# Two memory chains and two attention sweeps: from stages of their own to shared stages on five and three PSUM banks

## The chip, the cores and the metric

One core of a Trainium2 chip runs the whole program. The metric is the device time of one execution in microseconds (us). All executions told of here were fast, the undisturbed state. "Half clock" and "full clock" are the two values, 0.50 and 1.00, that the trace records for the clock granted to TensorE.

## The reference, cut to what matters

The program computes `g*a + (1-g)*b` for 2048 tokens of 576 features and the gradients of eleven inputs. Branch `a` is a plain attention with 32 heads of 18 features over one shared key and value. Branch `b` walks through 64 segments of 32 tokens, and each segment's eight memory rows are the output of the segment before.

```python
def _A_ref(x, wq, wk, wv, wo):
    q = (x @ wq) ...                       # 32 heads of 18
    k = x @ wk;  v = x @ wv                # one shared head
    p = softmax(q @ k.T * Dh ** -0.5)
    return (p @ v) ... @ wo
def _B_ref(x, mem0, Wq, Wk, Wv, Wo, seg_len):
    mem = mem0
    for s in range(n_seg):                 # 64 steps, strictly one after the other
        h = concatenate([mem, xs], axis=1) # 8 memory rows + 32 tokens
        q, k, v = ...                      # 32 heads of 128
        o = softmax(mask(q @ k.T)) @ v ... @ Wo
        mem = o[:, :M, :]
        outs.append(o[:, M:, :])
# out, vjp = jax.vjp(...): forward and all gradients
```

In the kernel the attention of `a` with its gradients is two *sweeps* of 1024 iterations each, an iteration being one 128x512 tile of scores for two heads. The memory recurrence of `b` is two *chains* of 64 steps, one forward and one backward. A sweep depends on no chain and a chain on no sweep.

## The kernel before

Each stage has its own pools, opened and closed one after the other, so no stage overlaps the next:

```python
                with SB("a2s") as a2s, PS("a2p") as a2p:
                    k.a_pass1(a1k, a2s, a2p)                 # first sweep
        with SB("a3k") as a3k, SB("a3s") as a3s, PS("a3p") as a3p:
            k.a_pass2(a3k, a3s, a3p)                         # second sweep
        # ... a_out, loads, b_proj_x cut ...
                with SB("cfs") as cfs, PS("cfp") as cfp:
                    k.b_chain_fwd(bw, cfs, cfp)              # forward chain
        # ... transposed weights, b_bulk cut ...
            with SB("rk") as rk, SB("rs") as rs, PS("rp") as rp:
                k.load_WoT(rk)
                k.b_chain_bwd(rk, rs, rp)                    # backward chain
```

One iteration of the first sweep. Its PSUM tiles come in pieces of 512 fp32 columns, one bank each, eight in all: three for S (the scores), two pairs for dP (the products with the output gradient) and one for the accumulator acc. E is the exponential of S, W the product of dP and E:

```python
                for kt in range(NTT):
                    k0 = kt * P
                    S = [psum.tile([P, 512], F32, name="a_S", bufs=3) for _ in range(2)]
                    dP = psum.tile([P, 2, 512], F32, name="a_dP", bufs=2)
                    for i in range(4):
                        r = slice(32 * i, 32 * i + 32)
                        dst = S[i][:, :] if i < 2 else dP[:, i - 2, :]
                        self.mm(dst, lhsT=self.KV[r, k0:k0 + P], rhs=QD[r, :], tp=(32 * i, 0))
                    Et = sp.tile([P, 2, 512], BF16, name="a_E", bufs=3)
                    Wt = sp.tile([P, 2, 512], BF16, name="a_W", bufs=3)
                    for i in range(2):
                        nc.scalar.activation(Et[:, i, :], S[i][:, :], ACT.Exp, scale=SCALEA)
                    nc.vector.tensor_tensor(out=Wt[:], in0=dP[:], in1=Et[:], op=ALU.mult)
                    # two acc matmuls of Et and two of Wt, 128x64 tiles side by side: cut
```

The second sweep is built alike, with b_S, b_dP, b_E, b_dS and four acc matmuls of 32 columns of the array. The last product of each backward chain step and the copies after it:

```python
            ph = psum.tile([P, 1024], F32, name="r_ph", bufs=1)
            for (lo, hi) in ((0, 512), (512, D)):
                for wi in (2, 0, 1):
                    for u in range(8):
                        for g in range(4):
                            self.mm(ph[32 * g:32 * g + 32, lo:hi], lhsT=dT[:, wi, u, :], rhs=self.WT[wi][:, 8 * g + u, lo:hi],
                                    start=(wi == 2 and u == 0), stop=(wi == 1 and u == 7), tp=(0, 32 * g))
            hs = sp.tile([P, D], F32, name="r_hs", bufs=1)
            nc.vector.tensor_copy(hs[:, 0:256], ph[:, 0:256])
            nc.scalar.copy(hs[:, 256:D], ph[:, 256:D])
```

The softmax here doesn't subtract the row's maximum and nothing guards it: scores larger than these inputs give would overflow.

## Time and profile before

The time is 11398.7 us (median of 4 runs, 11384.2 to 11406.1). The stages, from the first and last starts of their tiles:

| stage | us | per iteration or step | granted clock |
|---|---|---|---|
| first sweep | 2037 | 1.99 | 0.83 |
| second sweep | 1464 | 1.43 | 0.50 |
| forward chain | 1468 | 22.9 | 0.75 |
| bulk attention of branch b | 2000 | - | 0.59 |
| backward chain | 1545 | 24.1 | 0.65 |
| all the rest | 2891 | - | - |

The prediction below shows the lines that carry this. TensorE's timeline in the second sweep (start us, duration, engine, line, operation, tiles, shapes, count):

```profile
2600.48 0.60 PE L66 MATMUL b_dP<-b_KV,b_QD 32*128 32x512 bf16 x2
2600.49 0.96 PE L66 MATMUL b_S<-b_KV,b_QD 32*128 32x512 bf16 x2
2601.37 0.61 PE L66 MATMUL b_acc<-b_dS,b_SD 128*32 128x512 bf16 x2
2601.38 0.61 PE L66 MATMUL b_acc<-b_E,b_SD 128*32 128x512 bf16 x2
```

The eight matmuls of an iteration stand in two *groups*: four row tiles (dP and S) start together, then four column tiles (acc). Matmuls of one group share the array at the same time; each group takes over 0.5 us at half clock. A group is what the prediction calls a slot.

```profile
8496.58 8.82 PE L66 MATMUL r_ph<-WT,r_dT 128*32 128x512 bf16 x192 [0.46 <-ACT r_dT L608]
...
8507.59 3.74 PE L66 MATMUL r_pj<-WoT,dm 128*32 128x512 bf16 x40 [0.28 <-DVE dm L627]
```

After the product (r_ph) TensorE waits for two copies, and the next step's 40 projections (r_pj) then take 3.74 us.

### The profile page before, as it was taken

The numbers are of one execution on the slowest core, as the hardware profiler recorded it, in microseconds if no ns is written. First come the engines' busy times: TensorE is split into PE (matmuls) and PEld (weight loads), VectorE is DVE, ScalarE is ACT, GpSimd is POOL, SyncE is SP. The second block draws the span as 40 slices with busy tenths as digits, with TensorE's granted clock in tenths as the row PEclk, the third lists the DMA queues.
The fourth block names the chain that finished last, engine by engine and source line by source line (L and its number), as shares of the span: only waits on it lengthen the run. The fifth ranks groups of instructions, "written<-read, shape, count | busy, mean of one in ns | idle before, by whom it ended". The sixth has DMA issues, their size and how long they took to land. (4 is left out here: it accounts for less than half of the span.)

```text
span 11405.0 us, 219104 instructions
## 1 busy us (share of the span) xinstructions
PE 8865.9 (78%) x91009; PEld 3869.9 (34%) x91416; DVE 4143.1 (36%) x5742; ACT 3592.5 (31%) x6629; POOL 1540.5 (14%) x2664
## 2 busy tenths in 40 slices
PE   6777777799999998888876666665777776655898
PEld 2222222211112444444443333333333333333344
DVE  5666666688886331212122222221111111111001
ACT  4666666677776331111121111110000001112000
POOL 2111111100000000000022222221111111112101
PEclk8888888655556997777755655666666668877999
DMA  1000000311112442222254444444222224445544
GB/s 66 9 9 9 9 9 9 96 49 49 46 49 85 175 172 43 44 44 43 43 164 114 111 118 114 111 117 121 55 55 54 55 60 125 124 116 188 169 149 137
DMA packets 929961, 945.24 MB, mean 83 GB/s; under 512 B 457193, under 2 KB 801458, under 8 KB 910146
## 3 DMA queue, kind: packets, MB, share of 16 engines
q1 hardware_dynamic: 859330, 714.18, 21.7%
q0 software_dynamic: 69632, 217.01, 6.9%
q8 instruction: 716, 11.73, 0.4%
q14 instruction: 283, 2.32, 0.1%
HBM read 558.16 MB, written 372.57 MB: 82 GB/s over the span
## 5 line engine op out<-in xcount | busy, mean ns | idle before, releaser
L948 DVE TENSOR_TENSOR a_W<-a_dP,a_E 128x1024 bf16<-128x1024 f32 x1024 | 1252.4, 1225 | 583.3 <-ACT a_E L947 483.8
L1035 DVE TENSOR_TENSOR b_dS<-b_dP,b_E 128x1024 bf16<-128x1024 f32 x1024 | 1231.3, 1223 | 211.3 <-PE b_S L66 163.1
L947 ACT ACTIVATE a_E<-a_S 128x512 bf16<-128x512 f32 x2048 | 1116.0, 595 | 445.8 <-PE a_S L66 385.6
L1034 ACT ACTIVATE b_E<-b_S 128x512 bf16<-128x512 f32 x2048 | 1111.1, 594 | 351.0 <-DVE b_dS L1035 243.2
L66 PE MATMUL b_S<-b_KV,b_QD 32*128 32x512 bf16 x2048 | 897.8, 588 | 25.0 <-DMA b_QD<-qd_dram 25.0
L66 PE MATMUL a_acc<-a_W,a_WK 128*64 128x512 bf16 x2048 | 471.0, 447 | 387.5 <-DVE a_W L948 387.1
L66 PE MATMUL b_acc<-b_E,b_SD 128*32 128x512 bf16 x2048 | 626.9, 608 | 4.3 <-DMA b_SD<-sd_dram 3.3
L66 PE MATMUL b_acc<-b_dS,b_SD 128*32 128x512 bf16 x2048 | 626.2, 607 | 4.3 <-DVE b_dS L1035 1.8
L66 PE MATMUL b_dP<-b_KV,b_QD 32*128 32x512 bf16 x2048 | 620.7, 603 | 0.0
L66 PE MATMUL r_ph<-WT,r_dT 128*32 128x512 bf16 x12288 | 562.0, 353 | 29.5 <-ACT r_dT L608 29.5
L66 PE MATMUL a_S<-a_QD,a_KV 32*128 32x512 bf16 x2048 | 539.4, 443 | 44.6 <-ACT a_QD L922 43.1
L66 PE MATMUL w_acc<-w_d,w_h 128*128 128x512 bf16 (+1 forms) x2352 | 523.1, 380 | 37.5 <-DMA w_d<-dqx_dram 34.8
L66 PE MATMUL a_acc<-a_E,a_VK 128*64 128x512 bf16 x2048 | 520.2, 441 | 28.9 <-ACT a_E L947 25.8
L679 DVE COPY y_T<-y_pt 128x512 bf16<-128x512 bf16 x384 | 151.3, 422 | 934.8 <-PE y_pt L71 920.5
L66 PE MATMUL a_dP<-a_QD,a_KV 32*128 32x512 bf16 x2048 | 455.6, 441 | 0.0
L66 PE MATMUL y_pdx<-WT,y_T 128*128 128x64 bf16 (+1 forms) x2976 | 426.5, 289 | 24.1 <-ACT y_dx L685 10.9
L66 PEld LDWEIGHTS <-a_WK 128*64 128x64 bf16 x2048 | 195.1, 111 | 687.5 <-issue 680.0
L66 PE MATMUL c_pm<-c_oT,WoN 128*128 128x8 bf16 (+1 forms) x10080 | 340.3, 173 | 38.4 <-DVE c_oT L282 27.0
L66 PEld LDWEIGHTS <-r_dT 128*32 128x32 bf16 x12288 | 256.4, 109 | 334.9 <-issue 217.6
L66 PEld LDWEIGHTS <-b_SD 128*32 128x32 bf16 x4096 | 120.6, 101 | 731.1 <-issue 725.5
L66 PEld LDWEIGHTS <-WoN 128*128 128x128 bf16 (+1 forms) x10080 | 338.1, 114 | 50.9 <-issue 49.6
L66 PE MATMUL y_pk<-y_qB,y_dsB 128*128 128x512 bf16 x112 | 49.9, 446 | 391.9 <-DMA y_dsB<-dsmq_dram 391.9
(424 smaller groups left out, 13336.7 us busy)
## 6 DMA issues: line engine op xcount, KB each, us to landing
b_SD<-sd_dram SPq DMA_DIRECT2D x64, 512.0 KB
b_QD<-qd_dram SPq DMA_DIRECT2D x64, 512.0 KB
qx_dram<-p_tok SPq DMA_DIRECT2D x16, 1024.0 KB
qxT_dram<-p_tT SPq DMA_DIRECT2D x16, 1024.0 KB
kx_dram<-p_tok SPq DMA_DIRECT2D x16, 1024.0 KB
kxT_dram<-p_tT SPq DMA_DIRECT2D x16, 1024.0 KB
vx_dram<-p_tok SPq DMA_DIRECT2D x16, 1024.0 KB
vxT_dram<-p_tT SPq DMA_DIRECT2D x16, 1024.0 KB
```

The lines of the kernel that those rows point to most:

```text
L66: return self.nc.tensor.matmul(out, lhsT, rhs, start=start, stop=stop, tile_position=tp, skip_group_check=True)
L679: nc.vector.tensor_copy(tT[:], pt[:])
L947: nc.scalar.activation(Et[:, i, :], S[i][:, :], ACT.Exp, scale=SCALEA)
L948: nc.vector.tensor_tensor(out=Wt[:], in0=dP[:], in1=Et[:], op=ALU.mult)
L1034: nc.scalar.activation(Et[:, i, :], S[i][:, :], ACT.Exp, scale=SCALEA)
L1035: nc.vector.tensor_tensor(out=dS[:], in0=dP[:], in1=Et[:], op=ALU.mult)
```

## The change

Its intent: while a chain waits for softmaxes and copies, a sweep's independent matmuls can fill TensorE, so chain and sweep of each pair should cost little more than the larger of the two. The pools of a pair are open together, the chain is traced first and so goes first in the scheduler, and PSUM is split: three banks for the chain, five for the sweep.

```diff
+                with SB("a2k") as a2k, SB("cfs") as cfs, PS("cfp") as cfp, SB("a2s") as a2s, PS("a2p") as a2p:
+                    k.load_A_kv(a2k)
+                    k.b_chain_fwd(a2k, cfs, cfp)
+                    k.a_pass1(a2k, a2s, a2p)
 ... (cut)
-            with SB("rk") as rk, SB("rs") as rs, PS("rp") as rp:
+            with SB("rk") as rk, SB("rs") as rs, PS("rp") as rp, SB("a3k") as a3k, SB("a3s") as a3s, PS("a3p") as a3p:
                 k.load_WoT(rk)
                 k.b_chain_bwd(rk, rs, rp)
+                k.a_pass2(a3k, a3s, a3p)
 ... (in both sweeps; cut to the first)
-                    S = [psum.tile([P, 512], F32, name="a_S", bufs=3) for _ in range(2)]
-                    dP = psum.tile([P, 2, 512], F32, name="a_dP", bufs=2)
+                    S = [psum.tile([P, 512], F32, name="a_S", bufs=2) for _ in range(2)]
+                    dP = [psum.tile([P, 512], F32, name="a_dP", bufs=2) for _ in range(2)]
 ...
-                    nc.vector.tensor_tensor(out=Wt[:], in0=dP[:], in1=Et[:], op=ALU.mult)
+                    for i in range(2):
+                        nc.vector.tensor_tensor(out=Wt[i][:], in0=dP[i][:], in1=Et[i][:], op=ALU.mult)
 ... (last product of the backward step)
-            ph = psum.tile([P, 1024], F32, name="r_ph", bufs=1)
-            for (lo, hi) in ((0, 512), (512, D)):
+            for hf in range(2):
+                lo, hi = 288 * hf, 288 * hf + 288
+                ph = psum.tile([P, 288], F32, name="r_pj", bufs=2)
 ...
-            nc.vector.tensor_copy(hs[:, 0:256], ph[:, 0:256])
-            nc.scalar.copy(hs[:, 256:D], ph[:, 256:D])
+                nc.scalar.copy(hs[:, lo:hi], ph[:])
```

To make room, the rest was moved about: the Q and dO projections of the sweep became a stage of their own and are reloaded from memory; the output gradient's projection moved out of the bulk stage into the token projections; the second sweep loads 512 columns at a time; several tiles lost a buffer.

## The prediction

> **What bounds the kernel now.** I first read the page's busy shares (TensorE 78%, no other engine over 36%) and then the tiles' first and last starts, which split the run into stages. They run one after the other, so I asked for a table by stage. Columns: stretch, length, busy us of TensorE, weight loads, VectorE, ScalarE and GpSimd, then granted clock, DMA share, GB/s. In order: first sweep, second sweep, forward chain, bulk attention, backward chain.
>
> ```profile
> PEclk8888888655556997777755655666666668877999
> 113.00:2150.00 2037.00, 1482.96 (x9413) 467.27 (x9412) 1265.44 (x1088) 1298.36 (x2371) 298.18 (x808) 0.83 0.03 10
> 2150.00:3614.00 1464.00, 1434.15 (x8192) 254.56 (x8192) 1231.47 (x1026) 1113.17 (x2052) 13.30 (x24) 0.50 0.18 59
> 4250.00:5718.00 1468.00, 1259.27 (x24644) 694.34 (x24643) 291.86 (x643) 166.40 (x387) 132.55 (x190) 0.75 0.25 45
> 5830.00:7830.00 2000.00, 1321.80 (x9743) 725.16 (x9888) 502.57 (x1023) 360.96 (x656) 526.85 (x659) 0.59 0.43 119
> 7830.00:9377.00 1547.00, 1155.72 (x23752) 603.18 (x23751) 304.30 (x899) 116.36 (x320) 182.07 (x330) 0.65 0.27 56
> ```
>
> The sweeps use VectorE and ScalarE, the chains nearly only TensorE: the sum of a sweep and a chain is 3505 us (first pair) and 3011 us (second), and the change hopes to pay little more than the larger of each. Look at the clock: second sweep 0.50, with TensorE "busy" 98%. What sets an iteration there is VectorE:
>
> ```profile
> L948 DVE TENSOR_TENSOR a_W<-a_dP,a_E 128x1024 bf16<-128x1024 f32 x1024 | 1252.4, 1225 | 583.3 <-ACT a_E L947 483.8
> L1035 DVE TENSOR_TENSOR b_dS<-b_dP,b_E 128x1024 bf16<-128x1024 f32 x1024 | 1231.3, 1223 | 211.3 <-PE b_S L66 163.1
> L61 DVE CAST p_tok<-p_pb 128x512 bf16<-128x512 f32 x192 | 132.8, 692 | 327.4 <-PE p_pb L66 327.4
> ```
>
> 1.22 us of 1.43 us per iteration (1464/1024). Last, the timeline of TensorE, because the change alters how matmuls are grouped:
>
> ```profile
> 997.91 0.59 PE L66 MATMUL a_acc<-a_E,a_VK 128*64 128x512 bf16 x1 [0.26 <-ACT a_E L947]
> 998.43 0.60 PE L66 MATMUL a_S<-a_QD,a_KV 32*128 32x512 bf16 x1
> 998.96 0.64 PE L66 MATMUL a_acc<-a_E,a_VK 128*64 128x512 bf16 x1
> 999.53 0.61 PE L66 MATMUL a_dP<-a_QD,a_KV 32*128 32x512 bf16 x2
> ...
> 1000.50 0.64 PE L66 MATMUL a_acc<-a_W,a_WK 128*64 128x512 bf16 x2
> 1000.92 0.64 PE L66 MATMUL a_acc<-a_E,a_VK 128*64 128x512 bf16 x2
> ```
>
> One S matmul (32 rows of the array) between two acc matmuls takes 0.52 to 0.57 us, as much as a group of four S and dP together (999.53 on). So the array is paid by the group, a "slot": at clock 0.50 a slot from acc to S/dP is 0.56 us (second sweep 0.54), from S/dP to acc 0.53 (0.51); at clock 1.00 about 0.31.
>
> **What the Trainium skill says.** (1) "TensorE: Matmul & The Clock Gate", Part 3 (Packing small matmuls): matmuls on different row or column strips of the array run concurrently, and a weight load overlaps a running matmul only where its row group differs. The trace agrees: four row tiles start within 0.01 us, and acc to S costs more than its 0.43 us of streaming. (2) Same page, Part 1: the granted clock is half or full, set by activity over a window of about 3.4 us. The trace's records have only 0.5 and 1.0, in multiples of 3.413 us. (3) "Perfetto Trace Analysis", Optimization Strategy: interleaving regimes with different limits may help; that is this change's intent. (4) "PSUM — Partial Sum Buffer": 8 banks per partition, hence the split into 5 and 3.
>
> The trace tells more of the clock. For each 3.413 us record I summed the streaming time of its matmuls (512 columns: 0.213 us at full clock), each weighted by the share of the 128x128 array that it fills. At full clock, 264 of 264 records under 0.30 are followed by half clock, 0 of 1086 over 0.38. At half clock, 0 of 1241 records under 0.64 are followed by full clock, 181 of 181 over 0.78. So filled area counts, and once at half clock a loop must fill about three quarters of the array to leave it.
>
> **The change part by part.** The compiled order of the changed kernel's instructions decides here.
>
> Forward chain and first sweep. Each chain step holds some 25 sweep matmuls, in all 192 of 1024 iterations, in 1207 slots, nearly all between the softmax's matmuls and the next step. The other 832 iterations stand after the chain, alone, on five banks.
> - Chain step: 22.8 us now. 19 slots per step cost 5.9 us at 0.31 and 10 at 0.53. The waits that they fill are short: from the denominator matmul to the value matmuls 1.6 us, then 0.7 us before the output product, 0.35 before the next projection, 0.5 before the denominator. Following the new order: the value matmuls wait behind an acc that needs a VectorE product (0.69 us) queued after the chain's own, 2 us late; 0.6 and 1 us more at the other places. Step about 27 us, 64 of them: 1730 us.
> - Sweep alone: the order repeats [acc E, acc E] [S] [acc W] [dP, S] [acc W] [dP]: six slots instead of three (four S/dP; two acc; two acc), because with two banks each for S and dP every tile is refilled as soon as it is freed. 5150 slots counted. At half clock one iteration is 3x0.56 + 3x0.53 = 3.3 us, and its area is three full-array passes of 0.427 us in 3.3, or 0.39: under 0.64, so it stays at half clock. Even at full clock (6x0.31 = 1.9 us) the share is 0.34, at the edge, and the pause at each of the 52 block ends (copy and eight transposes, about 2.5 us) drops it. 832x3.3 + 130 = 2870 us. VectorE's two halves, 2x0.69 = 1.38 us, are hidden.
> - Together 4600 us + 20 of loads, against 3505.
>
> Backward chain and second sweep. On the SyncE queue the loads of all 64 chain steps stand ahead of the sweep's seventh, and a queue is served in order, so the sweep gets only six loads of 4 iterations: 24 iterations stand before or in the first two steps, and 999 after the chain.
> - Chain: 1547 us, + 25 because the products now share the two r_pj banks (r_ph waits for one more copy, 0.4 us x 64).
> - Sweep alone: [acc] [dP, S] [acc, acc, acc] [dP, S]: four slots instead of two, 2x0.54 + 2x0.51 = 2.10 us; area 2x0.427/2.1 = 0.41, half clock. The loop through one dP bank (product 0.69, acc 0.54, matmul 0.61, signals 0.15) is 2.0 us and does not add. 999x2.13 = 2130 us against 1464.
> - Together 3700 us against 3011.
>
> Elsewhere.
> - The Q/dO projections of the sweep become a stage: 64 x (five dense slots of 0.22 and one with waits of 0.5, 1.6 us) = 105 us (before, 4.4 us per block within the sweep).
> - dO moves from bulk to the token projections. One of three projections is 590/3 = 197 us, and building WoT moves (22 us), with a stage end of 25 us: +222.
> - Bulk loses five matmuls, four transposes and two copies per group: of 13.2 us a group the wait for x_dO and its transpose (2 us) and two WoT matmuls ahead of x_o's transpose (0.8): 10.5 us, x128 = -350 us.
> - Delta rows leave through one queue at the first sweep's end: +40. Second history: +13. The weight stage loses WoT: -20.
>
> Sum: 11400 + (4620-3505) + (3700-3011) + 105 + 222 - 350 + 33 + 90 for the added stage edges = 13300 us.
>
> **The rivals.**
> - Full overlap: each pair costs its larger limit. VectorE 1417 + 292, ScalarE about 1600, TensorE about 1800 in the first pair, 2000 each with friction: about 9400 us. Stage shares speak for it (VectorE 62%, TensorE 86% in opposite stages); the compiled order speaks against it, as it is fixed and each queue is served in order.
> - No overlap but a full clock in the lone sweeps: 832x1.95 and 999x1.5 us: about 11600 us. For it: in the first sweep six slots at full clock keep TensorE streaming 0.67 of the time. Against it: in the second sweep now, TensorE streams for 0.84 of a record, with area 0.60, and the clock stays half for 1400 us.
> - The chain's matmuls keep the clock up. They do so only inside the chain, where its output product (160 matmuls of 8 columns, area under 0.3) drops it every step.
> - DMA as the bound: 0.43 share in bulk rises to an estimated 0.6. I expect it hidden.
>
> **Range and chances.** Unsure: slot length in the lone sweeps (5% of 5000 is 250 us), step growth (2 us x 64 = 130), bulk (150), edges (100): about 350 together, so 12650 to 13900 holds it 8 times in 10. A loss is lost only if the clock or the order reading fails: faster 0.03, same 0.04, slower 0.93.
>
> **What would show it.** After the forward chain, some 2850 us with TensorE above 95% busy at clock 0.50, VectorE near 42%, six starts of groups 0.5 us apart per iteration. In the backward chain no b_ instructions after the second step; then about 2130 us at 0.50. VectorE products x2048 at 690 ns. Bulk near 1650 us. It is wrong if the clock in the lone sweeps exceeds 0.6, if single S and acc matmuls overlap, or if the chain steps stay under 24 us.

## The result, and the profile after

The changed kernel takes 12947.8 us (median of 4 runs: 12857.0, 12870.1, 13025.5, 13026.1). The ratio to the kernel before is 1.136, with a 95% interval of 1.126 to 1.146: slower by 13.6%. Here and below a ratio is the mean time of one kernel's fast runs over that of the other's of the same rounds, so it isn't quite the ratio of the medians quoted. The times come in two pairs some 160 us apart; the profiled execution (13023.8 us) is of the slower pair.

The same table by stage, for the changed kernel (stretch, length, then busy us and instruction counts of TensorE, weight loads, VectorE, ScalarE, GpSimd; then granted clock, DMA share, GB/s). In order: forward chain with what it took in of the first sweep, first sweep alone, bulk, backward chain, second sweep alone in two parts.

```profile
1168.00:2872.00 1704.00, 1674.22 (x26205) 796.86 (x26205) 464.25 (x966) 449.02 (x861) 150.28 (x190) 0.80 0.21 40
2872.00:5820.00 2948.00, 2913.57 (x7107) 649.98 (x7107) 1159.49 (x1723) 1076.07 (x1824) 199.52 (x578) 0.50 0.03 8
5916.00:7590.00 1674.00, 978.61 (x8734) 577.91 (x8733) 461.14 (x892) 282.42 (x528) 586.22 (x760) 0.63 0.51 139
7645.00:8997.00 1352.00, 1007.79 (x23836) 677.85 (x23836) 291.52 (x855) 153.44 (x407) 167.39 (x316) 0.81 0.29 62
8997.00:9364.00 367.00, 339.18 (x1881) 109.94 (x1879) 311.24 (x470) 254.64 (x471) 12.44 (x11) 1.00 0.16 50
9364.00:11020.00 1656.00, 1655.68 (x6132) 318.36 (x6131) 1059.93 (x1533) 892.66 (x1534) 0.00 (x0) 0.50 0.10 31
```

Read the second line first: with 832 of its 1024 iterations still to do, the first sweep runs alone for 2948 us, which is longer than the whole first sweep before. TensorE is 99% busy and the clock is 0.50 throughout, while VectorE is at 39%. The timeline of TensorE in that stretch shows what it is busy with:

```profile
4200.10 0.60 PE L66 MATMUL a_dP<-a_QD,l_KV 32*128 32x512 bf16 x1
4200.11 0.60 PE L66 MATMUL a_S<-a_QD,l_KV 32*128 32x512 bf16 x1
4200.64 0.64 PE L66 MATMUL a_acc<-a_W,l_WK 128*64 128x512 bf16 x1
4201.21 0.60 PE L66 MATMUL a_dP<-a_QD,l_KV 32*128 32x512 bf16 x1
4201.74 0.64 PE L66 MATMUL a_acc<-a_E,l_VK 128*64 128x512 bf16 x2
4202.31 0.60 PE L66 MATMUL a_S<-a_QD,l_KV 32*128 32x512 bf16 x1
4202.84 0.64 PE L66 MATMUL a_acc<-a_W,l_WK 128*64 128x512 bf16 x1
```

The starts 4200.10, .64, 4201.21, .74, 4202.31 and .84 are six groups, 0.53 to 0.57 us apart, and the next iteration starts at 4203.41: 3.31 us. The eight matmuls are the same as before; four of the six groups hold a single one. No wait stands in these lines: the busy share reports a full engine, while the matmuls fill 0.38 of the array (mean of this stretch's clock records, counted as in the prediction).

In the chains the sweep's matmuls fill waits as intended, but only 192 iterations fit into the forward chain and some 24 stand before and in the first steps of the backward one. The backward step itself became shorter:

```profile
8302.23 7.91 PE L66 MATMUL r_pj<-WT,r_dT 128*32 128x288 bf16 x192 [0.51 <-ACT r_dT L597]
...
8311.76 2.68 PE L66 MATMUL r_pj<-WoT,dm 128*32 128x512 bf16 x40 [0.28 <-DVE dm L616]
```

The first four lines of the table below are the two pairs of stages, 3505 + 3009 us before and 4652 + 3375 after: +1513 of the +1619 us between the two profiled executions. The new projection stage (about +130 us), the moved projection (about +230) and the lighter bulk stage (-326) nearly cancel.

| stage, us | before | after |
|---|---|---|
| forward chain | 1468 | 1704 |
| first sweep (alone) | 2037 | 2948 |
| backward chain | 1545 | 1352 |
| second sweep (alone) | 1464 | 2023 |
| bulk | 2000 | 1674 |
| all the rest | 2891 | 3323 |

### The profile page after: what moved, and what is told of

Its sections match the earlier page's. It is cut to its first block, busy times and chain, and to the rows that moved or that the text cites. A ratio compares the mean times of both kernels' runs of the same rounds, so it can differ in the third digit from the quotient of the medians.

```text
span 13023.8 us, 226895 instructions
## 1 busy us (share of the span) xinstructions
PE 11157.7 (86%) x91416; PEld 4426.6 (34%) x91416; DVE 4385.8 (34%) x7822; ACT 3790.7 (29%) x6789; POOL 1577.9 (12%) x2644
## 5 line engine op out<-in xcount | busy, mean ns | idle before, releaser
L952 DVE TENSOR_TENSOR a_W<-a_dP,a_E 128x512 bf16<-128x512 f32 x2048 | 1408.0, 690 | 1727.0 <-PE a_S L66 1147.9
L1042 DVE TENSOR_TENSOR b_dS<-b_dP,b_E 128x512 bf16<-128x512 f32 x2048 | 1403.3, 691 | 673.6 <-PE b_dP L66 314.1
L66 PE MATMUL a_acc<-a_W,l_WK 128*64 128x512 bf16 x2048 | 1224.2, 605 | 3.2 <-DVE a_W L952 2.8
L66 PE MATMUL b_acc<-b_dS,b_SD 128*32 128x512 bf16 x2048 | 1135.4, 556 | 29.7 <-DVE b_dS L1042 2.3
L66 PE MATMUL a_S<-a_QD,l_KV 32*128 32x512 bf16 x2048 | 1133.5, 565 | 28.7 <-ACT a_tk L979 16.2
L66 PE MATMUL a_dP<-a_QD,l_KV 32*128 32x512 bf16 x2048 | 1147.8, 571 | 0.0
L66 PE MATMUL b_dP<-b_KV,b_QD 32*128 32x512 bf16 x2048 | 1127.3, 552 | 0.0
L66 PE MATMUL a_acc<-a_E,l_VK 128*64 128x512 bf16 x2048 | 706.6, 599 | 21.6 <-ACT a_E L950 19.7
L66 PE MATMUL r_pj<-WT,r_dT 128*32 128x288 bf16 x12288 | 483.4, 329 | 31.6 <-ACT r_dT L597 31.6
L66 PE MATMUL y_pdx<-WT,y_T 128*128 128x512 bf16 (+1 forms) x3072 | 432.3, 291 | 15.8 <-ACT y_dx L674 10.9
```

The source lines that it names most:

```text
L66: return self.nc.tensor.matmul(out, lhsT, rhs, start=start, stop=stop, tile_position=tp, skip_group_check=True)
L952: nc.vector.tensor_tensor(out=Wt[i][:], in0=dP[i][:], in1=Et[i][:], op=ALU.mult)
L1042: nc.vector.tensor_tensor(out=dS[i][:], in0=dP[i][:], in1=Et[i][:], op=ALU.mult)
```

## The experiments

The theory: what costs time is not the sharing but its price, that is five banks and 512-wide tiles in the sweeps, which break each iteration into more groups, and at that filling the clock stays at half. Rivals: the collision of chain and sweep; the banks alone; the tiles alone; the clock alone; the reloads.

| run | banks of the sweep, tiles, stages | median us | ratio to before |
|---|---|---|---|
| the change | 5, 512-wide, shared | 12947.8 | 1.136 |
| e1_unshared | 5, 512-wide, apart | 13656.5 | 1.199 |
| e8_unshared_8banks | 8, 512-wide, apart | 13174.2 | 1.155 |
| e9_shared_pairs | 5, 1024-wide, shared | 13043.6 | 1.144 |
| e2_unshared_wide | 8, 1024-wide, apart | 11016.9 | 0.967 |

### Sharing undone, all else kept

```diff
-                with SB("a2k") as a2k, SB("cfs") as cfs, PS("cfp") as cfp, SB("a2s") as a2s, PS("a2p") as a2p:
-                    k.load_A_kv(a2k)
-                    k.b_chain_fwd(a2k, cfs, cfp)
-                    k.a_pass1(a2k, a2s, a2p)
+                with SB("cfk") as cfk, SB("cfs") as cfs, PS("cfp") as cfp:
+                    k.b_chain_fwd(cfk, cfs, cfp)
+            with SB("a2k") as a2k, SB("a2s") as a2s, PS("a2p") as a2p:
+                k.load_A_kv(a2k)
+                k.a_pass1(a2k, a2s, a2p)
 ... (the second pair likewise)
```

> The changed kernel with the sharing alone undone: each sweep has its own stage after its chain, with the same five banks, the same 512-wide tiles and the same order inside. Theory (the five-bank, 512-wide layout of the sweeps costs the time, the sharing itself gives a little back): the forward chain goes back to about 22.8 us a step (1470 us in place of 1704), the 192 iterations that it had taken in go to 3.3 to 3.5 us each (+650 us), the backward chain stays at about 1350 us because nothing of its own is touched, the second sweep stays at about 2020. Sum: about +400 us over the changed kernel, 13250 to 13450 us. Rival (the collision of chain and sweep in one stage is what costs): the total falls, to 12700 us or less, with the sweeps below 2.5 us an iteration when they are alone.

Measured: 13656.5 us (13652.0 to 13667.7), 700 us more than with sharing. The two sweeps, alone:

```profile
2617.00:6256.00 3639.00, 3581.02 (x8720) 797.97 (x8720) 1423.71 (x2112) 1323.38 (x2242) 242.76 (x705) 0.50 0.03 7
9416.00:11630.00 2214.00, 2211.79 (x8192) 425.15 (x8193) 1416.32 (x2048) 1193.76 (x2051) 0.00 (x0) 0.50 0.10 32
```

The forward chain fell to 1426 us, and the first sweep is 3.55 us an iteration (3639/1024), the same as the 3.54 of the changed kernel's tail (2948/832). The rival of a collision falls: sharing itself is a gain. In the forward chain 192 iterations cost 1704 - 1426 = 278 us, or 1.45 each, less than half of what they cost alone. The total missed the expected 13250 to 13450 by 200 us because the second sweep took 2214 us, not 2020: alone in its stage it went at half clock from the start, its first key block (a quarter of the sweep) too, while in the changed kernel what the chain leaves of that block goes at full clock (the 367 us line above).

### Eight banks and wide tiles, not shared

The diff on the sharing-undone kernel puts the tiles and loops of the kernel before back into both sweeps (S with three banks, dP as two pairs, one 1024-wide product).

> As the run with the sharing undone, and each sweep has all eight banks again with the tiles of the kernel before (three banks for S, two pairs of banks for dP, one product of 1024 columns). Theory (banks and tile width are the loss): first sweep 1900 to 2050 us, second about 1460, forward chain about 1500, backward chain about 1350, the rest as in the changed kernel; total 11100 to 11350 us, so 0 to 2.5 per cent faster than the kernel before, by the lighter bulk stage and the faster backward chain. Rival (the sweep is slow for the reloads of its projections from memory, which this run keeps): over 12300 us.

Measured: 11016.9 us (11007.2 to 11023.3), 2640 us below the run with sharing undone, and 3.3% faster than the kernel before. First and second sweep:

```profile
2607.00:4378.00 1771.00, 1372.22 (x8720) 425.86 (x8720) 1260.26 (x1088) 1215.64 (x2241) 241.95 (x703) 0.87 0.07 15
7551.00:8987.00 1436.00, 1429.80 (x8192) 253.59 (x8192) 1239.90 (x1024) 1112.81 (x2051) 0.00 (x0) 0.50 0.15 48
```

The total is a little below the range expected, because the first sweep with its projections ready-made takes 1771 us rather than 1900 to 2050. The reloads, which this run keeps, are not the loss. Banks and tiles together are worth 1868 us in the first sweep and 778 in the second, which is the whole difference (2646 of 2640).

### Banks or tiles: each alone

Eight banks with the split tiles, not shared:

```diff
-  name="a_S", bufs=2      name="a_dP", bufs=2      (512-wide; second sweep alike)
+  name="a_S", bufs=3      name="a_dP", bufs=4
```

> The changed kernel with the sharing undone and the split 512-wide tiles kept, but with eight banks: three for S, four for dP, one accumulator. It parts the two halves of what the run with wide tiles gained. If the number of banks is the loss: the sweeps come within 10 per cent of that run (first sweep 1771 us, second 1436), total 11050 to 11350 us. If the split tiles and the order that they give to the matmuls are the loss: the first sweep stays near 3600 us and the second near 2200, total over 13200 us. I expect the banks to carry most of it, but the two separate products of VectorE to keep more groups of matmuls apart: first sweep 1900 to 2600, total 11300 to 12300 us.

Measured: 13174.2 us (13162.6 to 13188.4). I had expected the banks to carry most of it, and that is wrong. The first sweep and its timeline:

```profile
2605.00:5745.00 3140.00, 3127.17 (x8720) 676.98 (x8720) 1367.15 (x2112) 1274.74 (x2241) 241.92 (x704) 0.50 0.04 9
```
```profile
4000.58 0.60 PE L66 MATMUL a_dP<-a_QD,l_KV 32*128 32x512 bf16 x1
4001.11 0.64 PE L66 MATMUL a_acc<-a_W,l_WK 128*64 128x512 bf16 x1
4001.68 0.60 PE L66 MATMUL a_dP<-a_QD,l_KV 32*128 32x512 bf16 x1
...
4002.22 0.63 PE L66 MATMUL a_acc<-a_W,l_WK 128*64 128x512 bf16 x1
```

Each line of dP has an S beside it. The iteration still comes in two halves, one head after the other: dP, S, acc, dP, S, acc, as I read it because two separate products of VectorE finish 0.7 us apart and the scheduler places what each frees. The last acc holds three matmuls for two column tiles and lasts 0.99 us. It all takes 2.63 us (4000.58 to 4003.21), still at half clock. The second sweep takes 2211 us, no less than with five banks. (In the run with wide tiles the order of its acc matmuls went back too, E before dS; what that alone does wasn't tested.)

Wide pairs in five banks, shared (one edit on the changed kernel; dP is a single pair, so a single buffer):

```diff
-                    dP = [psum.tile([P, 512], F32, name="a_dP", bufs=2) for _ in range(2)]
+                    dP = psum.tile([P, 2, 512], F32, name="a_dP", bufs=1)
 ... (one product of 1024 columns; E and W as pairs, two buffers; second sweep alike)
```

> The changed kernel, stages shared and five banks, but with the tiles of the kernel before inside them: dP as one pair of two banks (a single buffer), one product of 1024 columns, the matmuls of each iteration in four groups in place of six. If the six groups at half clock are what costs (3.3 to 3.5 us an iteration): 4 groups of 0.54 us or one round trip through the single dP pair (product 1.22 plus matmul 0.55 plus waits) give 2.0 to 2.4 us an iteration in the tail of the first sweep, 2948 us to 1700 to 2000, total 11700 to 12100 us. If five banks are the loss whatever the tiles, the single dP pair gives no gain: total within 3 per cent of the changed kernel, 12600 us or more.

Measured: 13043.6 us (13027.8 to 13057.1), as slow as the change. The first sweep's tail, and TensorE in it:

```profile
2795.00:5345.00 2550.00, 2187.21 (x7479) 590.17 (x7479) 1086.52 (x934) 1050.10 (x1921) 209.29 (x608) 0.50 0.04 10
```
```profile
4001.27 0.61 PE L66 MATMUL a_S<-a_QD,l_KV 32*128 32x512 bf16 x2
4002.15 0.64 PE L66 MATMUL a_acc<-a_W,l_WK 128*64 128x512 bf16 x2 [0.27 <-DVE a_W L952]
4002.72 0.61 PE L66 MATMUL a_dP<-a_QD,l_KV 32*128 32x512 bf16 x2
```

Now all groups hold two matmuls and there are four of them, but TensorE waits for VectorE in each iteration (the 0.27 in brackets), since one dP pair lets product and matmul only take turns: 2.56 us from one acc of W (3999.59) to the next (4002.15). The total hides two opposite effects. The first pair of stages gains 492 us (1610 + 2550 against 4652): an iteration of the tail costs 2.90 us in place of 3.54, though the chain took in only 146 iterations in place of 192. The second pair loses 506 us (1348 + 2533 against 3375), because there the round trip through the one pair, 2.53 us, is longer than the four groups' 2.16. So neither half of the layout does it alone. Of the layouts tried, only the one with two buffers of a *pair* kept an iteration in two or three groups; it has eight banks. Two pairs of dP with only two banks for S would take seven, and weren't tried.

### The clock: bursts of useless matmuls

If the tail runs at half clock only because its own matmuls fill too little of the array to lift it, a burst that fills the array should lift it. Forty 128x128 matmuls of 512 columns, never read, ahead of the last three of the four key blocks of the second sweep:

```diff
+            if kb >= 1:
+                heat = psum.tile([P, 512], F32, name="b_S", bufs=2)
+                for _ in range(40):
+                    self.mm(heat[:], lhsT=KV[:, 0:P], rhs=KV[:, 0:512])
             acc = psum.tile([P, 512], F32, name="b_acc", bufs=1)
```

> The changed kernel with 40 useless full-array matmuls (128x128 by 512 columns, into a bank of the sweep, never read) ahead of the second, third and fourth key block of the second sweep. Theory (those blocks run at half clock only because the pause at the block's end lets the clock fall and the sweep's own matmuls cannot lift it; full speed once lifted holds): each of the three blocks falls from about 553 us to 380 to 410, minus about 12 us for the burst, total about 430 us below the slower of the two times that the changed kernel shows, 12550 to 12650 us. Rival (the banks and their round trips set 2.16 us an iteration, the clock only follows): no block gets faster, and the total rises by 40 to 50 us.

Measured: 12904.0 us (12890.3 to 13046.2), not to be told from the changed kernel (both 1.136 times before). The third key block, then the fourth:

```profile
9911.00:10475.00 564.00, 562.79 (x2088) 109.92 (x2088) 354.06 (x512) 298.60 (x514) 0.00 (x0) 0.51 0.10 31
10475.00:10885.00 410.00, 378.32 (x2083) 122.91 (x2082) 341.15 (x512) 278.43 (x513) 0.00 (x0) 1.00 0.13 41
```

The fourth block did as expected, 410 us, so the round trips do not set 2.16 us; the second and third (563 and 564) did not, and the total missed the expected 12550 to 12650. The clock records of the trace, each 3.413 us, with the share of the time that matmuls stream and the share of the array that they fill, computed as in the prediction, show why (start us, clock, time, area):

```
second block                     fourth block
9348.8  1.00  0.99  0.99         10475.2  1.00  0.99  1.02
9352.2  1.00  0.96  0.93         10478.6  1.00  0.99  0.99
9355.6  1.00  0.48  0.21         10482.0  1.00  0.56  0.34
9359.0  0.50  0.78  0.41         10485.4  1.00  0.57  0.28
```

All three bursts lifted or held the clock. In the one record after it, while the pipeline of the sweep refills, the array was filled 0.21 in one case and 0.34 in the other (0.27 ahead of the third block, which also fell back), by where the burst happened to end in the record, and the clock fell or stayed.

The same burst also ahead of each of 51 blocks of 16 iterations in the first sweep's tail:

> As the run with bursts in the second sweep, and the same burst ahead of each of the 51 query blocks of the first sweep that run after the forward chain. Theory (the tail of the first sweep is at half clock for the same reason, and keeps full clock between two bursts): its 832 iterations go from 3.5 to 2.0 to 2.3 us, -1000 to -1250 us, against 51 bursts of 10 to 14 us (+500 to +700), so another 300 to 700 us below the run with bursts in the second sweep alone: 11900 to 12300 us. Rival A (six groups of matmuls an iteration hold too little work, and the clock falls back within a block): no gain and the bursts' cost on top, 13200 us or more. Rival B (round trips through the banks bound it): the same as A, but with the clock high and the iterations still 3.3 us.

Measured: 12638.6 us (12528.8 to 12707.2); its four times lie 180 us apart, and the expected 11900 to 12300 was too hopeful. In the profiled run 36 of the tail's 52 blocks take 43 to 45 us and the others 54 to 65. One of each kind:

```profile
2998.00:3041.00 43.00, 41.51 (x176) 14.19 (x176) 21.68 (x33) 20.66 (x35) 3.79 (x11) 1.00 0.04 8
```

At full clock a block is 43.1 us with 8.6 us of burst in it (40 matmuls 0.216 us apart), so 2.16 us an iteration in place of 3.54; the block from 3041 to 3104 took 63.2 us at a clock of 0.61. To test that the thin record after the burst decides, I put three more dummies ahead of each of the first four iterations after a burst:

```diff
+                    if p * 4 + qb >= 13 and kt < 4:
+                        for _ in range(3):
+                            self.mm(S[0][:, :], lhsT=self.KV[:, 0:P], rhs=self.KV[:, 0:512])
 ... (second sweep: if kb and p == 0 and qt < 4)
```

> The run with bursts in both sweeps, and three more useless full-array matmuls ahead of each of the first four iterations after a burst. In that run a quarter of the blocks of the first sweep, and the second and third of the second sweep, fell back to half clock in the record just after the burst, where the refilling pipeline streams only 0.48 to 0.57 of the time. Theory (it is this one thin record that loses the clock): every block of the first sweep takes 45 to 47 us, 51 x 46 = 2350 us in place of 2600, and all four key blocks of the second sweep 370 to 420, 1600 us in place of 1900; total 12000 to 12250 us, with no two groups of times. Rival (the pause at the block's end, or a limit on how long the clock is granted, drops it): the same share of blocks falls back, and the total is 12600 us or more.

Measured: 12237.4 us; three runs within 9 us of each other and one at 12083.0. The total stands at the upper edge of what was expected; the two groups of times did not wholly go.

```profile
2873.00:5308.00 2435.00, 2339.92 (x9638) 788.28 (x9737) 1118.92 (x1718) 1057.37 (x1820) 197.16 (x574) 0.99 0.04 10
```

Fifty-one of the tail's 52 blocks now take 46.6 to 48.6 us, and the last three key blocks of the second sweep 413 us each, all at full clock. What still varies is the first key block, which has no burst: in the profiled run it went at half clock (502 us). That is what one expects if the thin record loses the clock. The half clock is worth about 1.4 us of the 3.5 of an iteration (3.54 against 2.16). Set against the 1.73 us of the run with eight banks and wide tiles (1771/1024), it is 1.4 of the 1.8 us lost: the six groups cost time mainly by keeping the array too thinly filled to win the clock. With nearly all of both sweeps at full clock this kernel is still 7% slower than the one before, but some 600 us of that are the dummies themselves (an estimate: 54 bursts of 40, and 12 more each, 0.216 us apart). Without them it would stand at about 11630 us, 2% slower.

### A dummy in each iteration of the best run

In the run with eight banks and wide tiles the second sweep stays at half clock with a filled share of 0.64 to 0.72. One dummy per iteration should lift it:

```diff
+                    self.mm(S[0][:, :], lhsT=KV[:, 0:P], rhs=KV[:, 0:512])
                     for i in range(4):
                         r = slice(32 * i, 32 * i + 32)
```

> The run with eight banks, wide tiles and no sharing, with one useless full-array matmul (128x128 by 512 columns) per iteration of the second sweep, written into the S bank that the next matmul overwrites. In that run the second sweep streams a filled share of the array of 0.64 to 0.72 at half clock and never rises; the first streams 0.82 in the record before each rise. Theory (a filled share of about 0.75 lifts the clock): the dummy brings it to about 0.78, the clock rises to 1.00, and the sweep is then bound by VectorE's 1.22 us product: 1436 us to 1270 to 1310, total 10850 to 10900 us. Rival (the filled share is not what lifts it): the dummy only adds its 0.43 us at half clock to each iteration, +200 to +440 us, total above 11200 us.

Measured: 11258.3 us (11244.2 to 11265.5), 240 us slower than without. Second sweep and timeline:

```profile
7561.00:9225.00 1664.00, 1486.38 (x9214) 441.88 (x9214) 1253.69 (x1024) 1141.38 (x2051) 0.00 (x0) 1.00 0.13 41
```
```profile
8002.09 0.39 PE L66 MATMUL b_S<-b_KV 128*128 128x512 bf16 x1
8002.41 0.39 PE L66 MATMUL b_S<-b_KV,b_QD 32*128 32x512 bf16 x1
8002.73 0.39 PE L66 MATMUL b_acc<-b_dS,b_SD 128*32 128x512 bf16 x2
```

Both theory and rival were half right. The clock did rise to 1.00, so the filled share lifts it; yet the sweep grew from 1436 to 1664 us. Two things in the trace go with that. The dummy (first line) stands between S matmuls that had gone together, and the iteration now has four to five groups of 0.31 us. And the late S delays what follows: VectorE waits 374 us for E (8 us without the dummy) and TensorE 119 us for VectorE's products (under 1 us without). Which of the two sets the 1.63 us of an iteration wasn't tested.

### The backward chain: the split product alone

The kernel before with one edit, the product's halves of 288 columns (as in the diff of the change, in its own two r_ph banks):

> The kernel before with one edit: the last product of each backward memory step (r_ph, 576 columns) is cut in 288 and 288 in place of 512 and 64, each half copied by ScalarE as soon as it is done. Theory (this split is what makes the changed backward chain about 165 us faster than that of before, by hiding one copy and by keeping the clock up): the backward chain falls from 1545 us to 1370 to 1420 and the total to 11210 to 11280 us. Rival (the chain is faster for something else: single buffers, the smaller load of the transposed values, the shared banks): the total stays within 30 us of the kernel before.

Measured: 11189.4 us (11178.3 to 11193.0), 0.981 of before (95% interval 0.980 to 0.982), a larger gain than expected. The backward chain:

```profile
7825.00:9142.00 1317.00, 967.39 (x23736) 671.23 (x23735) 276.04 (x831) 139.78 (x383) 169.35 (x318) 0.83 0.31 64
```

It fell by 228 us, more than the 193 of the changed kernel, so the split is enough to explain all of it. Per step that is 3.6 us: the product takes 7.27 us for 8.82; the time from its end to the next matmul shrinks from 0.63 us to none, as the first half's copy is hidden; and the 40 projections after it take 2.67 us for 3.74. The clock of the stage went from 0.65 to 0.83. How much of this the clock does, and how much the evener widths, I did not separate.

### The queue of the second sweep's loads

The changed kernel with the loads of the second sweep issued by GpSimd:

```diff
-                        nc.sync.dma_start(QD[:], self.qd_dram[p][:, qt * P:qt * P + 512])
+                        nc.gpsimd.dma_start(QD[:], self.qd_dram[p][:, qt * P:qt * P + 512])
 ... (SD likewise)
```

> The changed kernel with the second sweep's loads issued from GpSimd in place of SyncE, so that they no longer stand behind the loads of all 64 backward steps. In the compiled order this puts 478 of the 1024 iterations of the second sweep ahead of the chain's end, some 60 matmuls a step, in place of 25 iterations in its first two steps. Theory (the queue's order is why the second pair of stages hardly overlapped, and an iteration taken into the chain costs about what it did in the forward chain, 282 us for 192, or 1.5 us): the backward chain grows from 1352 us to 1950 to 2150, the sweep alone shrinks from 2023 us to 1080 to 1180 at half clock; total 12600 to 12850 us, a small gain. Rival (taken in, an iteration costs as much as alone, because every group of sweep matmuls sits in front of the chain's): no gain, 12950 to 13300 us.

Measured: 12664.6 us (12660.9 to 12678.9), ratio 1.111. Backward chain with what it took in (the second sweep alone then took 1159 us):

```profile
7613.00:9496.00 1883.00, 1791.59 (x27478) 873.21 (x27476) 870.34 (x1765) 646.18 (x1319) 285.23 (x553) 0.79 0.30 66
```

Some 453 more iterations moved into the chain at (1883 - 1352)/453 = 1.17 us each, against 2.1 alone. The total is as expected. The chain, 1883 us, grew less than the 1950 to 2150 foreseen. Taken in, the sweep's groups fill waits of the chain, and they run at the clock of this stage, 0.79. Both make sharing pay; how much each gives wasn't parted.

### The best version

The run with eight banks and wide tiles, and one transfer of the backward chain moved from GpSimd to SyncE:

```diff
-            nc.gpsimd.dma_start(vxT[:], self.xTd["v"][tt][:, :, 32 * sl:32 * sl + 32])
+            nc.sync.dma_start(vxT[:], self.xTd["v"][tt][:, :, 32 * sl:32 * sl + 32])
```

> The fastest run so far (no sharing, eight banks, wide tiles) with one transfer of the backward chain (r_vxT) issued from SyncE in place of GpSimd, where its 1.68 us of issue stands ahead of a copy that the chain needs (r_dspad). Theory: about 1 to 1.5 us of each of 64 steps goes, 60 to 110 us, total 10900 to 10960 us. Rival (the copy waits for VectorE's r_dS anyway, or the SyncE queue becomes the bound): within 30 us of 11017.

Measured: 10948.4 us (10936.0 to 10952.4), 0.960 of before, as expected; the backward chain went from 1379 to 1287 us. This is the fastest version: the change's other parts without its sharing and its five banks, and with this transfer moved.

## Why the prediction was right or wrong

The direction, the range and the main mechanism were right; the point, 13300 us, was 350 too high (276 against the profiled execution, from which the stages below are read). By its own steps:

- **Forward chain.** 1730 us predicted with 192 iterations taken in, 1704 measured. Right.
- **First sweep alone.** 2870 us of six groups at half clock predicted, 2948 measured, clock 0.50, groups 0.53 to 0.57 us apart. Right. The reason given, "with two banks each for S and dP every tile is refilled as soon as it is freed", was only half of it: with eight banks and the same tiles the sweep still took 3140 us.
- **Backward chain.** This is the step that failed: "1547 us, + 25" against 1352. It counted the wait for one more copy and overlooked that the even split hides a copy and shortens product and projections; the split alone took 228 us from the kernel before.
- **Second sweep alone.** 2130 us at half clock predicted, 2023 measured. Four groups were right: starts at 9999.66, 10000.19, 10000.74 and 10001.27 us, the next iteration at 10001.82, 2.16 us. The size was off because the rest of the first key block (367 us) went at full clock, so that the mean clock of the lone sweep, 0.59, came just under the 0.6 that the prediction had named as a sign of being wrong. The rule behind it, that a full clock falls in every record filled under 0.30, came from the kernel before; in the changed kernel 146 of 198 full-clock records between 0.25 and 0.30 were followed by full clock. (The count takes 0.213 us for 512 columns at full clock, half of what the traces show at half clock; dense matmuls start 0.216 us apart.)
- **Elsewhere.** Bulk -350 predicted, -326 measured; the new projection stage 105 against about 130; the moved projection 222 against about 230; edges and the rest 123 against about 70 (what is left of the 432 us by which the rest of the table grew). Right in sum, with errors of both signs (+24, +25, +8, -53), so partly by luck.
- **The rivals.** Full overlap failed as argued: the compiled order leaves 832 and about 1000 iterations outside the chains. Moving the loads showed that for the second pair the queue's order does part of it: with them moved, 477 of the 1024 went in. The figure given for this rival, 9400 us, doesn't follow from its own terms: 11400 - 3505 - 3011 + 2 x 2000, with the 100 elsewhere, is about 9000. The rival of a full clock in the lone sweeps named rates of 1.95 and 1.5 us that a full clock does give (six groups of 0.33 us in the run with the tended bursts; 367 us for about 235 iterations), but the tail doesn't reach it unaided.

What stays open, besides what is said above: no profile was taken of a 12860 us execution of the changed kernel. The 160 us to the others is about what one key block gains at full clock (553 us against some 400), and the mean clock of those runs is higher, 0.715 and 0.716 against 0.698 and 0.700; that they differ by one block is likely, not shown.

## What to carry to other kernels

Before two stages share PSUM, count how many groups each iteration's small matmuls fall into once the banks are split: here the array was paid by the group, and pairs of tiles that fill and empty together, with a second buffer, kept groups whole where single tiles didn't. A busy share of 99% at half clock was no sign of useful work; look at the order of the matmuls and at how much of the array they fill. Filling a chain's waits pays (1.2 to 1.5 us for iterations that cost 2.1 to 3.5 alone), but what stands outside the chain runs under the layout that the sharing forced, and here that was most of it.

## What the Trainium skill lacked or had wrong

- "TensorE: Matmul & The Clock Gate", Part 1, The HAM clock gate: it ties the clock to how busy the array has recently been and says next to nothing of what counts as busy. Over all thirteen traces here, the filled share of the array separates better than the share of time that matmuls stream, at half clock above all. At half clock, 0 of 17310 records of 3.413 us filled under 0.55 were followed by full clock and 1637 of 1637 over 0.80; at full clock, 0 of 1891 under 0.20 stayed and 15236 of 15236 over 0.40; between these limits both occur. (Counts move by up to 8% with how the streaming is laid into the records; no exception appears either way.) So keeping the clock takes far less than winning it. A sweep 99% busy but filled 0.38 stayed at half clock for 2948 us.
- Same page, Part 3, Packing small matmuls: it gives the gain of packing but no figure for breaking a pack: where row and column tiles alternate, each group takes 0.53 to 0.57 us at half clock and 0.31 to 0.34 at full, even for a single matmul of 512 columns.
- "DMA: Bandwidth & Descriptors", Issuing engines are not separate DMA queues: it says that issuing from several engines only saves the time to initiate. Here the second sweep's loads stood behind those of all 64 chain steps on SyncE; issued by GpSimd, they brought some 453 iterations forward and took about 280 us off (12947.8 to 12664.6, medians).
